# One mask for the 16 heads of a unit, and the output decay of a unit moved behind the mask of the next

## The chip, the cores and the metric

The kernel runs on one core of a Trainium2 chip. Its engines work side by side, each through its own instructions in order: TensorE (PE; its weight loads are shown as PEld), VectorE (DVE), ScalarE (ACT), GpSimd (POOL) and SyncE (SP), which here issues the DMA transfers. They wait for one another through semaphores. The metric is the device time of one execution in microseconds (us); the median of the runs counts.

## What is computed

Inputs are r, k, v, w, a, b for 4 batches x 8 heads, 768 time steps and 40 columns. For each head a 40x40 state is carried through time, and its output is then the input of a small layer of four attention experts, of which each token uses two:

```
for t in range(768):
    y[:, :, t] = einsum('bhd,bhde->bhe', r_t, state)
    Sa = einsum('bhde,bhe->bhd', state, a_t)
    state = state * w_t[:, :, None, :] - einsum('bhd,bhe->bhde', Sa, b_t)
    state = state + einsum('bhd,bhe->bhde', v_t, k_t)
x = y.transpose(0, 2, 1, 3).reshape(4, 768, 320)
```

Each expert e is then a causal softmax attention over x with wq[e], wk[e], wv[e] and wo[e]; the four are summed with the weights of a gate that keeps about the two largest.

## The kernel before

`recurrence` computes y, `moe` the experts. Time is cut into 24 chunks of 32 steps (c); four chunks make a group (w, six of them; cw is the chunk within the group). Within a chunk the recurrence is turned into matrix products: a unit is one chunk of 16 heads (G is 0 or 1), so there are 48 units, u = 2c + G. For each unit `unit(u)` gives seven pieces:

- `s_k`: transposes of the prepared keys KB (one for both units of a chunk), copied to LS by ACT (L373)
- `s_g` (L380): products with the state R1, copied to GT by ACT (L383)
- `s_u` (L388): products of GT with the inverted triangle TT, copied into rows 32 to 63 of R2 by ACT (L390)
- `s_v` (L395): transposes of R2, copied to VU by ACT (L396)
- `s_f` (L401): eight products (two instructions each) of VU with RB into one PSUM bank `p_f`; VectorE multiplies them by the triangular mask into R2 (L404), the first four products by one instruction and the last four by a second
- `s_y` (L412): 16 products (two instructions each) of LS with R2 into the fixed PSUM tile PY: the next state and the output of the chunk. ACT copies the state part to R1 (L424); in the last chunk of a group VectorE does it with a factor (L422). VectorE multiplies the output part by the decays SC into XT (L425, "the decay"). In the last chunk of a group four DMAs store XT to xT in DRAM (L430)
- `s_t` (L438): transposes of the new state, copied to LS by ACT (L440)

The main loop (L527) goes through steps n and takes, by the table MAIN, `s_v` of unit n-1, `s_t` of n-3, `s_k`, `s_g` of n, `s_f` of n-1, `s_u` of n and `s_y` of n-1. Behind every piece it puts the jobs of a hand-written table (SIDE, SIDE1, SIDE2): the preparation of the next group in `prep` (scans and products on VectorE, flags on ACT, the kb products L294 on PE, which VectorE moves out of PSUM with a mask in L295; loads of EW, EA and EK by SP in L208; stores Ld in L299) and the inversion of the triangles in `invert` (L324 and L326 on VectorE and GpSimd, which read MT and LT, loaded from Ld in L312 and L313). Each engine's order is that of this program text (`manual_schedule`), so whatever stands behind a waiting instruction on its engine waits too. The state goes from `s_y` of a unit over L424 to `s_g` of the unit two later. PSUM tiles named `ps` and `pw` have two buffers each, PY one.

Of the kernel before, what the change touches and what calls it, by code (L numbers as in the profile page):

```python
# [9 lines left out]
OP = mybir.AluOpType  # L10
# [131 lines left out]
def recurrence(tc, ctx, I, xT, FL, CM, early, tail=None, KP=(11, 11, 11, 11, 11, 11)):  # L142
    nc = tc.nc
# [4 lines left out]
    V, A, T, PL = nc.vector, nc.scalar, nc.tensor, nc.gpsimd  # L148

    def ps(shape):  # L150
        return pp.tile(shape, F32, name="ps", tag="ps", bufs=2)
# [10 lines left out]
    ident, mask, maskn = CM[:, 0:128], CM[0:64, 128:160], CM[0:64, 160:192]  # L162
# [32 lines left out]
    hd = lambda t, d: t.rearrange("p (h d) -> p h d", d=d)  # L195
# [55 lines left out]
            zero(t[96:128, 0:1280])  # L251
            A.activation(hd(t[64:104, 0:1280], 40), ident[64:104, None, 64:104].to_broadcast([40, 32, 40]), AF.Copy)

    pm, behind = [0, False], []

    def prep(i):

# [98 lines left out]
    def unit(u):  # L356
        c, G = divmod(u, 2)
        w, cw = divmod(c, 4)
        h0 = 16 * G
        gl, tt, ls, r1, r2, rb, sc = GF[w % 2], TF[w % 2], LS[c % 2], R1[c % 2], R2[c % 2], RB[c % 2], SC2[(w * 2 + G) % 6]  # L360
        gt, vu, xt = GT[G], VU[0], XT[G]
# [36 lines left out]
        def s_f():  # L398
            p_f = ps([64, 16, 32])
            for P in range(8):  # L400
                T.matmul(p_f[:, 2 * P:2 * P + 2], vu[:, P, :], rb[:, 8 * G + P, :], start=True, stop=True)  # L401
                if P % 4 == 3:
                    x = slice(8 * (P // 4), 8 * (P // 4) + 8)
                    V.tensor_tensor(hd(r2[0:64, 1280 + 512 * G:1792 + 512 * G], 32)[:, x], p_f[:, x],  # L404
                                    mask[:, None, :].to_broadcast([64, 8, 32]), op=OP.mult)
        def s_y():
            a = r2[:, 0:40]
            for P, s in PS:
                h = h0 + 2 * P + s
                m = bass.AP(a.tensor, a.offset + 40 * h, [a.ap[0], [1280 - 8 * h, 2], [1, 40]])  # L410
                o = 80 * (P % 4)
                T.matmul(PY[64 * s:64 * s + 40, P // 4, o:o + 80].rearrange("q (x d) -> q x d", x=2), ls[:, h, :], m, start=True, stop=True,  # L412
                         tile_position=(0, 64 * s))
            py = PY[:, :, 0:320].rearrange("q b (p x d) -> q b p x d", p=4, x=2)
            for s in range(2):
                q = slice(64 * s, 64 * s + 40)
                if c < 23:
                    o = rn[64:104, 832 * G:832 * G + 832].rearrange("q (b p e) -> q b p e", b=2, p=4)[:, :, :, 64 * s:64 * s + 40]
                    st = py[q, :, :, 0]
                    if cw == 3:  # L420
                        pn = PC2[((c + 1) // 4 * 2 + G) % 6]
                        V.tensor_tensor(o, st, pn[q, :, :, None].to_broadcast([40, 2, 4, 40]), op=OP.mult)  # L422
                    else:
                        A.activation(o, st, AF.Copy)  # L424
            V.tensor_tensor(xt[:, :, 32 * cw:32 * cw + 32].rearrange("q (b p) t -> q b p t", b=2), py[0:104, :, :, 1, 0:32],  # L425
                            sc.rearrange("q b (p c) t -> q b p c t", p=4)[:, :, :, cw, 0:32], op=OP.mult)
            if cw == 3:
                for g in range(2):
                    for s in range(2):
                        nc.sync.dma_start(xT.rearrange("b (p s e) t -> b s e p t", s=2, e=40)[2 * G + g, s, :, :, 128 * w:128 * w + 128],  # L430
                                          xt[64 * s:64 * s + 40, 4 * g:4 * g + 4])
        def s_t():
            if c == 23:
                return
# [4 lines left out]
            def copy(s):  # L439
                A.activation(ln[64:104, h0 + s:h0 + 16:2].rearrange("q (b p) e -> q b p e", b=2),  # L440
                             p_t[64 * s:64 * s + 40, :, 0:416].rearrange("q b (p e) -> q b p e", p=4)[:, :, :, 64:104], AF.Copy)
            behind.extend(lambda s=s: copy(s) for s in range(2))
        return dict(k=s_k, g=s_g, u=s_u, v=s_v, f=s_f, y=s_y, t=s_t)


    jobs = {}
    NU = 48
    MAIN = [("v", -1), ("t", -3), ("k", 0), ("g", 0), ("f", -1), ("u", 0), ("y", -1)]

    def at(n, s, *fs):  # L450
        n = max(n, 0)
        x = ("f" if s <= 3 else "u") if n % 2 == 0 else ("u" if s <= 2 else "y")
        q = jobs.setdefault((n // 2, x), [])
        q.extend(((n, s), f) for f in fs)
# [5 lines left out]
    P = [prep(i) for i in range(24)]  # L460
# [63 lines left out]
            for z in part.split():  # L524
                at(n, k, lambda z=z: seq(z))
    pm[1] = True
    for n in range(NU + 1):  # L527
        if n == 40:
            early.close()
            for k, s, f in tail(KB[4:]) if tail else []:  # L530
                at(k, s, f)
        for x, d in MAIN:
            if x == "k":
                if n % 2 == 0 and n < NU:
                    units[n if n % 4 == 0 else n - 1]["k"]()
            elif 0 <= n + d < NU:
                units[n + d][x]()
            while x == "g" and behind:
                behind.pop(0)()
            if n and x == ("y" if n % 2 else "k"):  # L540
                load_c((n + 3) // 2, 2 * (n % 2))
            if n and n % 2 == 0 and x == "y":
                load_c((n + 3) // 2, 1)
            for _, f in sorted(jobs.get((n, x), []), key=lambda z: z[0]):
                f()
# [427 lines left out]
```

## Time and profile before

| | before |
|---|---|
| runs | 750.51, 739.98, 752.2 us; median 750.51 |
| profiled execution | 748.43 us, span of the trace 746.6 |
| PE / PEld busy | 586.2 (79%) / 508.2 (68%) |
| DVE busy | 491.1 (66%) |
| ACT busy | 463.6 (62%) |
| POOL busy | 336.0 (45%) |
| chain that ended last | PE 45%, DVE 22%, ACT 14%, DMA 7% |

All times of the profile are from the start of the span. Busy time is time in which an engine executes; matmuls are pipelined, so PE's is no measure of its peak. PEclk is the clock that TensorE was granted, as a share of full speed. A wait is put down to the engine that released it last. The chain that ended last is followed back from the last instruction of the execution.

### The profile page before, as it was taken

Reading aid. Unit: us, or ns where it says so; the run is one execution under the profiler, and the core shown is the slowest. Engines: PE = TensorE matmul, PEld = TensorE weight load, DVE = VectorE, ACT = ScalarE, POOL = GpSimd, SP = SyncE. Lnnn points to the kernel's source line nnn. Section 1 sums busy time; section 2 is a strip of 40 time slices with the busy share of each in tenths; the row PEclk is TensorE's granted clock in tenths of the full one; section 3 lists DMA queues with packets and bytes.
Section 4 is the critical chain, followed back from the end, with each engine's and each line's share of the span. In section 5 each row is a group of like instructions: output and inputs, shape, how many; then the busy total and the mean of one; then the engine's idle time right before and its main releaser. Section 6 shows DMA issues by size and latency. Waiting matters only on the chain.

```text
span 746.6 us, 21791 instructions
## 1 busy us (share of the span) xinstructions
PE 586.2 (79%) x8801; PEld 508.2 (68%) x8801; DVE 491.1 (66%) x1155; ACT 463.6 (62%) x1018; POOL 336.0 (45%) x512
## 2 busy tenths in 40 slices
PE   4530677785778767877798888879989989999996
PEld 4520666685668667866687777778778777877774
DVE  8899777745755586568656533239898678658751
ACT  6793477555666756675666766746656556656753
POOL 5465288217812683168307600114556244532641
PEclk9565699978889988998899999999999999999999
DMA  7861573457445843684445283143113212111101
GB/s 186 202 155 40 124 172 94 111 103 185 106 123 112 204 105 102 131 207 106 107 84 157 84 203 102 34 138 95 45 51 93 51 42 78 54 40 43 36 28 49
DMA packets 88548, 78.10 MB, mean 105 GB/s; under 512 B 54776, under 2 KB 72952, under 8 KB 88440
## 3 DMA queue, kind: packets, MB, share of 16 engines
q1 hardware_dynamic: 88296, 76.54, 41.5%
q8 instruction: 71, 1.16, 0.7%
q14 instruction: 37, 0.30, 0.1%
q10 hardware_dynamic: 144, 0.10, 0.0%
HBM read 56.17 MB, written 14.16 MB: 94 GB/s over the span
## 4 chain that ended last, share of the span: by engine, by line
PE 45%; DVE 22%; ACT 14%; DMA 7%; issue 5%; SPq 0%; POOL 0%; ACTq 0%; DVEq 0%; POOLq 0%
PE ot L857 5%; PE sc L809 4%; PE ps L401 4%; PE pt L731 4%; DMA EK<-in_EK 4%; PE pt L839 4%; PE pt L866 3%; DVE MT L326 3%; PE py L412 3%; PE pt L750 3%; PE ps L380 3%; DVE TP L324 3%; PE pw L294 2%; PE pw L368 2%; PE ps L388 2%
## 5 line engine op out<-in xcount | busy, mean ns | idle before, releaser
L831 POOL TENSOR_TENSOR P<-P,m 128x128 f32<-128x128 f32 (+2 forms) x96 | 87.7, 935 | 103.0 <-DVE m L827 51.8
L401 PE MATMUL ps<-RB,VU 128*64 128x64 f32 x768 | 70.3, 240 | 51.1 <-DVE R L404 47.5
L404 DVE TENSOR_TENSOR R<-ps,CM 64x256 f32<-64x256 f32 x96 | 39.9, 415 | 101.9 <-PE ps L401 101.9
L401 PEld LDWEIGHTS ps<-RB,VU 128*64 128x64 f32 x768 | 57.7, 150 | 59.0 <-DVE R L404 54.3
L326 POOL TENSOR_TENSOR MT<-MT,TP 128x84 f32<-128x84 f32 (+13 forms) x169 | 85.8, 508 | 13.2
L383 ACT ACTIVATE GT<-ps 32x320 f32<-32x320 f32 x96 | 41.0, 428 | 70.5 <-PE ps L380 69.7
L820 ACT ACTIVATE P<-sc,m 128x128 f32<-128x128 f32 (+2 forms) x96 | 60.8, 634 | 31.9 <-DVE m L819 25.9
L819 DVE TENSOR_REDUCE m<-sc 128x1 f32<-128x128 f32 (+2 forms) x96 | 59.4, 622 | 27.3 <-PE sc L812 25.8
L412 PE MATMUL py<-R,LS 128*40 128x80 f32 x1536 | 71.8, 249 | 3.7 <-ACT LS L373 3.7
L390 ACT ACTIVATE R<-ps 32x320 f32<-32x320 f32 x96 | 41.2, 429 | 43.6 <-PE ps L388 42.6
L809 PE MATMUL sc<-ks,qs 128*128 128x384 f32 (+4 forms) x256 | 64.4, 353 | 4.5 <-ACT P L820 4.2
L412 PEld LDWEIGHTS py<-R,LS 128*40 128x40 f32 x1536 | 63.3, 128 | 5.1 <-ACT LS L373 5.0
L324 POOL TENSOR_TENSOR TP<-LT,MT 128x220 f32<-128x220 f32 (+9 forms) x100 | 52.1, 521 | 7.8
L839 PE MATMUL pt<-CM,P 128*128 128x128 f32 x336 | 51.9, 276 | 2.4 <-ACT pt L845 2.0
L368 PE MATMUL pw<-CM,KB 104*128 104x104 f32 x192 | 24.8, 278 | 36.4 <-DVE GL L295 24.6
L294 PE MATMUL pw<-AB,KB 104*64 104x64 f32 x672 | 49.5, 238 | 1.9 <-DVE GLe L295 1.8
L388 PE MATMUL ps<-GT,TT 128*33 128x40 f32 x1536 | 46.9, 217 | 4.1 <-DVE GL L295 4.1
L809 PEld LDWEIGHTS sc<-ks,qs 128*128 128x128 f32 x256 | 41.2, 191 | 12.1 <-ACT P L820 9.8
L395 PE MATMUL pw<-CM,R 66*80 66x66 f32 x384 | 33.0, 232 | 20.2 <-issue 14.6
L396 ACT ACTIVATE VU<-pw 80x512 f32<-80x512 f32 x48 | 28.5, 594 | 32.6 <-PE pw L395 31.8
L294 PEld LDWEIGHTS pw<-AB,KB 104*64 104x64 f32 x672 | 47.2, 153 | 2.2 <-DVE GLe L295 2.0
L368 PEld LDWEIGHTS pw<-CM,KB 104*128 104x128 f32 x192 | 19.8, 152 | 40.5 <-DVE GL L295 24.7
(151 smaller groups left out, 1460.2 us busy)
## 6 DMA issues: line engine op xcount, KB each, us to landing
RB<-in_RB SPq DMA_DIRECT2D x24, 320.0 KB
EK<-in_EK SPq DMA_DIRECT2D x18, 416.0 KB
ks<-ks SPq DMA_DIRECT2D x32, 192.0 KB
R<-in_VG SPq DMA_DIRECT2D x24, 208.0 KB
EW<-in_EA SPq DMA_DIRECT2D x18, 214.5 KB
R<-in_VT SPq DMA_DIRECT2D x48, 80.0 KB
R<-in_RT SPq DMA_DIRECT2D x24, 160.0 KB
xT<-XT SPq DMA_DIRECT2D x48, 80.0 KB
```

Source lines behind the costliest of these rows:

```text
L294: T.matmul(p_a[:, p, cc, :], kb[0:104, n, :], AB[0:104, n, :], start=True, stop=True)
L324: return [lambda: e.tensor_tensor(tmp, row[:, None, :].to_broadcast([128, m, n]), M[:, r0:r0 + m, j][:, :, None].to_broadcast([128, m, n]) ...
L326: lambda: e.tensor_tensor(o, o, tmp, op=OP.add)]
L368: T.transpose(p_k[:, g, 128 * p:128 * p + 104], KB[(w * NG + 2 * G + g) % NKB][0:104, p * 4 + cw:p * 4 + cw + 2, :].rearrange("q c k -> q ...
L388: T.matmul(p_u[64 * s:64 * s + 33, P], tt[:, o:o + 33], gt[:, P, s], start=True, stop=True, tile_position=(0, 64 * s))
L401: T.matmul(p_f[:, 2 * P:2 * P + 2], vu[:, P, :], rb[:, 8 * G + P, :], start=True, stop=True)
L412: T.matmul(PY[64 * s:64 * s + 40, P // 4, o:o + 80].rearrange("q (x d) -> q x d", x=2), ls[:, h, :], m, start=True, stop=True, tile_positi ...
L809: T.matmul(ps[:, c, 0:cw], QS[b][:, e, o], KS[b][:, e, z, k], start=(z == 0), stop=(z == 1 and not last), skip_group_check=True)
L819: V.tensor_reduce(m[:, 0, t:t + 1], ps[:, 0:ch, 0:cw], axis=AX.XY, op=OP.max, negate=True)
L820: later(DE, lambda: A.activation(pv, ps[:, 0:ch, 0:cw], AF.Exp, bias=m[:, 0, t:t + 1], accum_out=m[:, 1, t:t + 1]))
L831: PL.tensor_tensor(P[:, 0:n], P[:, 0:n], m[:, 3, t:t + 1].to_broadcast([128, n]), op=OP.mult)
L839: T.transpose(p[:, 128 * y:128 * y + 128], st["P"][t][:, 128 * c:128 * c + 128], ident)
```

## The change

`s_f` masks all 16 heads of the unit with one VectorE instruction behind the eighth product. `s_y` no longer issues the decay and the stores: it puts them into a list `late`, which the main loop empties right behind `s_f` of the next step. The loop runs one step longer, for the last decay.

```
-    pm, behind = [0, False], []
+    pm, behind, late = [0, False], [], []
...
                 T.matmul(p_f[:, 2 * P:2 * P + 2], vu[:, P, :], rb[:, 8 * G + P, :], start=True, stop=True)
-                if P % 4 == 3:
-                    x = slice(8 * (P // 4), 8 * (P // 4) + 8)
-                    V.tensor_tensor(hd(r2[0:64, 1280 + 512 * G:1792 + 512 * G], 32)[:, x], p_f[:, x],
-                                    mask[:, None, :].to_broadcast([64, 8, 32]), op=OP.mult)
+            V.tensor_tensor(hd(r2[0:64, 1280 + 512 * G:1792 + 512 * G], 32), p_f, mask[:, None, :].to_broadcast([64, 16, 32]), op=OP.mult)
...
-            V.tensor_tensor(xt[:, :, 32 * cw:32 * cw + 32].rearrange("q (b p) t -> q b p t", b=2), py[0:104, :, :, 1, 0:32],
-                            sc.rearrange("q b (p c) t -> q b p c t", p=4)[:, :, :, cw, 0:32], op=OP.mult)
-            if cw == 3:
...
+            def decay():
+                V.tensor_tensor(xt[:, :, 32 * cw:32 * cw + 32].rearrange("q (b p) t -> q b p t", b=2), py[0:104, :, :, 1, 0:32],
+                                sc.rearrange("q b (p c) t -> q b p c t", p=4)[:, :, :, cw, 0:32], op=OP.mult)
+                if cw == 3:
...
+            late.append(decay)
...
-    for n in range(NU + 1):
+    for n in range(NU + 2):
...
                 units[n + d][x]()
+            while x == "f" and late:
+                late.pop(0)()
```

The lines of the changed kernel move with it: the mask is L402, `s_y`'s products L409, the factor copy L419, ACT's state copy L421, the decay L423, the stores L428.

On TensorE, one step of the main loop with its waits (R and RB are a chunk's buffers, LS the weights of `s_y`). Before:

```order
L401 MATMUL ps<-RB_127,VU_126 64x64 [waits DMAHW3_49,Activation_49]
L401 MATMUL ps<-RB_127,VU_126 64x64 x3
L401 MATMUL ps<-RB_127,VU_126 64x64 [waits DVE_49]
L401 MATMUL ps<-RB_127,VU_126 64x64 x3
L388 MATMUL ps<-GT_132,TT_118 33x40 [waits PE_49,Activation_49]
L388 MATMUL ps<-GT_132,TT_118 33x40 x15
L412 MATMUL py<-R_124,LS_120 40x80 [waits DMAHW4_49,Activation_49]
L412 MATMUL py<-R_124,LS_120 40x80 [waits Activation_49]
L412 MATMUL py<-R_124,LS_120 40x80 x5
L412 MATMUL py<-R_124,LS_120 40x80 [waits DVE_49]
```

and of the change, the same step:

```order
L401 MATMUL ps<-RB_127,VU_126 64x64 [waits DMAHW3_49,Activation_49]
L401 MATMUL ps<-RB_127,VU_126 64x64 x7
L388 MATMUL ps<-GT_132,TT_118 33x40 [waits PE_49,Activation_49]
L388 MATMUL ps<-GT_132,TT_118 33x40 x15
L409 MATMUL py<-R_124,LS_120 40x80 [waits DMAHW4_49,DVE_49,Activation_49]
L409 MATMUL py<-R_124,LS_120 40x80 [waits Activation_49]
L409 MATMUL py<-R_124,LS_120 40x80 x14
```

The wait for VectorE in the middle of `s_f` is gone, and the one in `s_y` has moved from its eighth product to its first.

On VectorE, the end of a chunk group, steps with kb products (`-` before, `+` the change; XT is the decay's output, GLe that of the kb products' mask, R that of the mask or of the state's factor copy):

```order
-L404 TENSOR_TENSOR R_125<-ps,CM 64x256 x2
+L402 TENSOR_TENSOR R_125<-ps,CM 64x512
+L423 TENSOR_TENSOR XT_130<-py,SC_93 104x8x32
 L279 TENSOR_TENSOR AB_111<-EA_82,SC_97 40x16x32
 L295 TENSOR_TENSOR GLe<-pw,CM 64x4x128 x2
-L422 TENSOR_TENSOR R_122<-py,PC_88 40x8x40 x2
-L425 TENSOR_TENSOR XT_129<-py,SC_92 104x8x32
+L419 TENSOR_TENSOR R_122<-py,PC_88 40x8x40 x2
 L270 SCALAR_TENSOR_TENSOR SUF_85<-EW_81,D_79 104x528
 L272 COPY PC_86<-SUF_85 104x4
 L274 RECIPROCAL D1P_84<-PC_86 104x4
```

Two masks have become one, the decay of the unit before follows it, and the unit's own decay no longer stands behind the state's factor copy and ahead of the scan.

On SP's queue, the stores of one XT at the end of a chunk group (TT, R, Ld and EK are loads and stores of the jobs and of `load_c`):

```order
 L332 DMA TT_119<-Td_136 32x32x32 x4
-L430 DMA xT<-XT_129 40x4x128 x4
-L350 DMA R_125<-in_VT 32x640
-L299 DMA Ld_133<-GLe 32x32x32
-L348 DMA R_123<-in_VG 32x1664
+L350 DMA R_125<-in_VT 32x640
+L299 DMA Ld_133<-GLe 32x32x32
+L348 DMA R_123<-in_VG 32x1664
+L428 DMA xT<-XT_129 40x4x128 x4
 L208 DMA EK_83<-in_EK 104x1024
```

The four stores have moved behind three other transfers and stand directly ahead of the load of EK.

## Rows read from the trace of the kernel before

**Rows 1.** Waits of all engines: engine, line, whom for: us in all, times, longest.
```profile
PE ps L401 <- DVE R L404: 47.5, 48, 5.4
```

**Rows 2.** Timeline, an undisturbed step: start us, us, engine line op out<-in, [idle before].
```profile
442.38 0.65 PE L401 MATMUL ps<-RB,VU 128*64 128x64 f32 x8
442.60 0.87 ACT L383 ACTIVATE GT<-ps 32x320 f32<-32x320 f32 x2 [0.77 <-PE ps L380]
443.07 0.42 DVE L404 TENSOR_TENSOR R<-ps,CM 64x256 f32<-64x256 f32 x1 [1.91 <-PE ps L401]
...
443.54 0.62 PE L401 MATMUL ps<-RB,VU 128*64 128x64 f32 x7 [0.51 <-DVE R L404]
...
443.94 0.22 PE L388 MATMUL ps<-GT,TT 128*33 128x40 f32 x1
...
444.58 0.24 PE L412 MATMUL py<-R,LS 128*40 128x80 f32 x1
...
444.62 1.28 PE L412 MATMUL py<-R,LS 128*40 128x80 f32 x31
```

**Rows 3.** Timeline of VectorE: the first and the last of the 15 late masks.
```profile
89.62 0.39 DVE L404 TENSOR_TENSOR R<-ps,CM 64x256 f32<-64x256 f32 x1
...
417.67 0.41 DVE L404 TENSOR_TENSOR R<-ps,CM 64x256 f32<-64x256 f32 x1
```

**Rows 4.** Timeline, a step whose mask is late.
```profile
199.86 0.68 PE L401 MATMUL ps<-RB,VU 128*64 128x64 f32 x8
...
202.46 0.41 DVE L404 TENSOR_TENSOR R<-ps,CM 64x256 f32<-64x256 f32 x1
...
204.78 0.35 PE L412 MATMUL py<-R,LS 128*40 128x80 f32 x1
...
204.90 1.85 PE L412 MATMUL py<-R,LS 128*40 128x80 f32 x31
```

**Rows 5.** Windows: length; busy of PE, PEld, DVE, ACT, POOL; PEclk; DMA; GB/s.
```profile
202.90:206.80 3.90, 3.88 (x74) 3.77 (x75) 2.47 (x7) 1.61 (x4) 3.16 (x9) 0.59 0.23 54
442.30:446.00 3.70, 3.19 (x97) 2.94 (x92) 0.83 (x2) 2.62 (x7) 0.00 (x0) 1.00 0.79 210
```

**Rows 6.** Groups by shape (busy, mean ns | idle), then timeline of VectorE.
```profile
L295 DVE TENSOR_TENSOR GL<-pw,CM 64x512 f32<-64x512 f32 x22 | 14.6, 677 | 6.7 <-PE pw L294 6.7
...
218.54 1.27 DVE L295 TENSOR_TENSOR GL<-pw,CM 64x512 f32<-64x512 f32 x2
...
439.69 1.01 DVE L422 TENSOR_TENSOR R<-py,PC 40x320 f32<-40x320 f32 x2 [1.28 <-PE py L412]
...
440.73 0.43 DVE L425 TENSOR_TENSOR XT<-py,SC 104x256 f32<-104x256 f32 x1
```

**Rows 7.** Timeline of ScalarE in a step with `s_k`: first and last of eight rows.
```profile
342.50 0.87 ACT L383 ACTIVATE GT<-ps 32x320 f32<-32x320 f32 x2 [1.73 <-PE ps L380]
...
348.37 0.59 ACT L396 ACTIVATE VU<-pw 80x512 f32<-80x512 f32 x1
```

**Rows 8.** Timeline of VectorE behind a second mask.
```profile
212.61 0.42 DVE L404 TENSOR_TENSOR R<-ps,CM 64x256 f32<-64x256 f32 x1 [0.77 <-PE ps L401]
212.95 0.22 DVE L326 TENSOR_TENSOR MT<-MT,TP 128x75 f32<-128x75 f32 x1
```

**Rows 9.** Timeline of VectorE, a load it waits for.
```profile
258.56 1.76 DVE L284 TENSOR_TENSOR KB<-EK,SUF 104x512 f32<-104x512 f32 x2 [0.32 <-DMA EK<-in_EK]
```

**Rows 10.** Timeline of TensorE, `s_v` behind a step with kb products.
```profile
231.94 0.63 PE L395 MATMUL pw<-CM,R 66*80 66x66 f32 x8 [1.87 <-issue]
```

**Rows 11.** Timelines of SP's queue, VectorE and GpSimd around one EK load.
```profile
233.82 0.39 SPq L208 DMA_DIRECT2D EK<-in_EK  x1
...
236.95 0.42 DVE L404 TENSOR_TENSOR R<-ps,CM 64x256 f32<-64x256 f32 x1 [4.52 <-PE ps L401]
...
238.64 3.08 POOL L281 TENSOR_TENSOR KB<-EK,SUF 104x1024 f32<-104x1024 f32 x1 [22.09 <-DVE R L404]
...
248.47 0.16 POOL L315 MEMSET MT<- 128x32 f32 x1 [5.47 <-DMA MT<-Ld]
```

More of the change, by code (lines that the diff above doesn't have):

```diff
@@ L424, in s_y @@
                         A.activation(o, st, AF.Copy)
-            V.tensor_tensor(xt[:, :, 32 * cw:32 * cw + 32].rearrange("q (b p) t -> q b p t", b=2), py[0:104, :, :, 1, 0:32],
-                            sc.rearrange("q b (p c) t -> q b p c t", p=4)[:, :, :, cw, 0:32], op=OP.mult)
-            if cw == 3:
[L428 to L431, printed above, removed]
+            def decay():
+                V.tensor_tensor(xt[:, :, 32 * cw:32 * cw + 32].rearrange("q (b p) t -> q b p t", b=2), py[0:104, :, :, 1, 0:32],
+                                sc.rearrange("q b (p c) t -> q b p c t", p=4)[:, :, :, cw, 0:32], op=OP.mult)
+                if cw == 3:
+                    for g in range(2):
+                        for s in range(2):
+                            nc.sync.dma_start(xT.rearrange("b (p s e) t -> b s e p t", s=2, e=40)[2 * G + g, s, :, :, 128 * w:128 * w + 128],
+                                              xt[64 * s:64 * s + 40, 4 * g:4 * g + 4])
+            late.append(decay)
         def s_t():
```

## The prediction

> **What bounds the kernel now.** I read the page first (busy shares, then the 40 slices), then the list of waits, then the timeline of single steps in the part in which the 48 units run. No engine is busy throughout there: the units are a chain that goes round TensorE (PE), ScalarE (ACT) and VectorE (DVE), one unit per step. So the change is worth what it takes out of a step's chain, not what it takes off DVE's busy time.
>
> The list of waits has one entry that belongs to this change alone [rows 1]: PE waits 48 times for L404, 47.5 us in all, once in every step. It stands in the middle of `s_f`: the fifth product may not be written into the PSUM bank while DVE masks the first four.
>
> A step without other trouble is [rows 2]. Set its first product at 0. The first four products take 0.65, the mask starts at 0.69 and ends at 1.11, the second four start at 1.16 (0.05 after the mask), `s_u` at 1.56, and `s_y` at 2.20, as soon as `s_u` is issued. The second mask lies beside `s_u`. The wait there is 0.51; 48 of those would be 24.5 us, so the other 23.0 us come from steps in which DVE comes late to the mask. There are 15 such steps, with the first mask 0.3 us or more late: the first and the last of these masks are in [rows 3]. [rows 4] is one: the mask starts at 202.46 instead of 200.55. In the stretch behind it the granted clock is 0.59, where the undisturbed step has 1.00 [rows 5], so nearer to 1.2 than to 2.4 GHz, and `s_y` takes 1.85 us.
>
> **The change part by part.** *One mask.* The 16 product instructions now run in one piece. Eight take 0.40 to issue (443.54 to 443.94), and a mask starts 0.69 behind the start of the eight that it waits for, so it starts at 0.40 + 0.69 = 1.09. `s_u` can start when both GT copies are done, 443.47 and 0.05, at 1.14: it gains 0.42. The price of a 64x512 mask is that of L295, the same form with a mask factor: 0.677 us [rows 6].
>
> *The decay behind it.* It is one DVE instruction of 0.42 per unit, of the unit before. It reads PY, which `s_y` writes, and the rows of the built order show the one wait of `s_y` on DVE moved to its first matmul, with the decay ahead of it. So `s_y` waits for mask and decay. How soon the decay follows is bounded on both sides: two L295 in a row take 1.27 for 0.68 each, so the second starts 0.59 behind the first; L425 behind L422 starts 0.03 after its end, 0.71 for a mask [rows 6]. I take 0.59, because mask and decay, like two L295, both start at partition 0, while the second L422 starts at partition 64. The Trainium skill, page "VectorE: DVE Perf Modes", section "Two Vector instructions with no wait between them", says that a Vector instruction is held until the earlier ones are finished when its operands start in another group of 32 partitions than the last ones in that memory, and otherwise starts earlier; both rows agree, and by it the value is also 0.59.
>
> So behind a mask `s_y` can start 0.59 + 0.42 + 0.05 = 1.06 later. In an undisturbed step that is 1.09 + 1.06 = 2.15 (2.27 by the other bound) against 2.20: **nothing gained, -0.05 to +0.07**. The 0.42 that `s_u` gains is spent in front of `s_y`. I count 0.
>
> *Late steps.* Before, `s_y` starts 1.51 behind the first mask in a fast step (443.07 to 444.58) and 2.32 in a slow one (202.46 to 204.78); now 1.06. By the timeline 7 of the 15 are slow: 7 x 1.26 = 8.8. Of the other 8, four are steps with `s_k`, in which ACT works without a gap from the GT copy to the VU copy that the next `s_f` waits for (342.50 to 348.96, [rows 7]); a sooner `s_y` gives nothing there. The other four: 4 x 0.45 = 1.8. Together **10.6**.
>
> *DVE gets free sooner.* From the first mask to DVE's next work it was 0.42 + 0.77 + 0.34 = 1.53 [rows 2, 8]; now it is 0.59 and the decay, which is only moved. That is 0.94 per step, plus any wait of the decay. It counts only where the next mask is late from DVE's own work: the steps whose first products stand at about 118, 200, 275 and 349 us. The one at 200 is 1.9 late [rows 4], the others by the timeline about as much or more; I take 0.94 and a further 0.35 from the step before, whose own lateness or decay wait goes too: 4 x 1.3 = **5.2**. Where a load makes DVE late, as EK does at 258.56 [rows 9], nothing comes earlier.
>
> *Steps with kb products (L294) between `s_u` and `s_y`.* In the last three steps of a chunk group L294 fills PE between the two, so `s_y` is held by PE, not by DVE, and the 0.42 of `s_u` stays: 8 steps x 0.42 = 3.4. In 8 steps DVE had the decay in front of the L295 that empty the PSUM which the next `s_v` waits for (1.87 us at 231.94, [rows 10]); it goes from there: 8 x 0.34 = 2.7. Together **6.1**.
>
> *Last unit.* No `s_u` stands there, so `s_y` could start at 1.56 and now starts at 2.15: **-0.6** (a loss). The last decay stands where it stood.
>
> *The stores, on SP's queue.* The decay of every fourth pair issues four stores of xT. They move too: behind VT, Ld and VG, and they now wait for a decay behind the next unit's mask. EK is issued behind them. Before, EK was issued at 233.82 and POOL's KB started 4.8 later. Now: mask at 236.95 + 0.40, decay done 1.01 later at 238.4, four issues at the 0.39 that EK's own takes, EK at about 240, **6 us later**. What covers it: POOL's next fixed date is MT at 248.47, 9.8 behind KB's start, with KB itself (3.08) and one more product between [rows 11]. So the cover is about used up, and the EA load behind that product may slip, and with it the mask behind 258.56. The second set of stores moves out from in front of RB, RT and EA, which helps EA. In three windows the cost lies between 0 and 3 x 6; I take 1.3 each, since the cover in the row is nearly as long as the delay: **-4**.
>
> **Sum.** 10.6 + 5.2 + 6.1 - 0.6 - 4 = 17.3 us. The profiled execution took 748.43 (span 746.6); that gives 731.1, and I predict **731 us**. Against the median of the runs shown, 750.51, it would be 2.6% less, against the profiled run 2.3%.
>
> **The rivals.**
> *A: the wait only moves.* ACT or POOL set the step wherever DVE and PE come sooner, so that the 5.2 and the 6.1 are lost. For it: ACT's gapless step [rows 7]. Against it: in the late slow steps ACT waits for PE behind the mask. 748.4 - 10.6 + 4.6 = 742.4. Within 2%.
> *B: the load chain gives it all back (slower).* EK 6 us late passes on to the Ld store and the MT load behind it, and in all four windows to the mask that waits for EK. 4 x 6 lost against 21.9 - 0.6 = 21.3 gained: 748.4 - 21.3 + 24 = 751.1. It decides from 21.3 / 4 = 5.3 us per window on. Against it: the 6.75 between the end of KB and MT.
> *C: the clock comes back.* With shorter waits the slow steps stay at the upper level. `s_y` then takes 1.28 as in [rows 2] instead of the 1.85 of [rows 4]: 0.57 in each of 7 steps, 4 us, and without the loss on loads 731.1 - 8 = 723. The Trainium skill, page "TensorE: Matmul & The Clock Gate", section "Part 1: The HAM clock gate", says that the throttled clock is the default and activity releases it, which would be this; the 0.59 behind the late mask agrees. Against C: three of the seven are late from loads, and there the wait in front of `s_y` remains.
>
> **How the numbers follow.** Forecast (725 to 738) 0.47; A 0.33; C 0.12; B 0.08. The range reaches to C at 722 and to just past A at 744; beyond it lie B and the tails of A and C, 2 in 10. Differences of 2% are about what a measurement of this kernel can tell from no change (its three runs lie between 739.98 and 752.2). Faster by over 2% means under 735.5: most of the forecast's case (0.39), C (0.12) and little of A: 0.52. Slower by over 2% means over 765.5, for which B would have to cost 9.6 us in each window: 0.05 with what I may have overlooked. Within 2%: 0.43.
>
> **What would show it.** The waits of L401 on the mask are gone from the list. A wait of `s_y` (L409) on DVE appears, about 0.4 us in undisturbed steps, 1 us or more in late ones, and `s_y` starts 2.15 to 2.27 behind the first product there. The mask takes 0.68, the decay starts 0.59 behind it and no longer waits for L421. The undisturbed steps keep their period; the steps at 118, 200, 275 and 349 us lose 2 to 3 us each. EK is issued about 6 us later against its step, and POOL's KB with it. I am wrong if undisturbed steps get longer by more than 0.1 (then the decay is dearer than here), if the masks behind EK come later against their step by more than 2 us (B), or if the late steps lose less than 1 us (A).

## The result and the profile after

The change is worth about 1%: 736.19 us (median of 20 runs) against 742.85 us of the kernel before, timed in turn with it (20 runs); the ratio is 0.9894, with a 95% interval from 0.986 to 0.9927. That is within 2%. (The ratio leaves out six runs of the change that lie more than 1.5% above its fastest one; the two medians alone would give 0.991.) Predicted were 731 us, a range from 722 to 744, and chances of 0.52 for faster, 0.43 for the same and 0.05 for slower.

The profiled execution took 742.62 us, near the upper end of what the changed kernel needs (729.09 to 744.53). Since two of its executions differ by more than the change brings, I read two traces of it: this first one, and a second one of 730.14 us (below). From the page of the first, the span, the busy times (behind each engine its share of the span and its instructions) and the granted clock in the 40 slices (tenths of full speed):

```profile
span 740.5 us, 21727 instructions
PE 596.9 (81%) x8801; PEld 517.7 (70%) x8801; DVE 491.1 (66%) x1107; ACT 463.3 (63%) x1018; POOL 341.0 (46%) x512
PEclk8675688889789977898799999999999999999999
```

The line that the change aimed at, PE waiting 48 times for the first half mask [rows 1], is gone. The groups of the three lines concerned (busy, mean ns of one | idle ahead of them, and what ended it):

```profile
L401 PE MATMUL ps<-RB,VU 128*64 128x64 f32 x768 | 60.8, 239 | 3.7 <-ACT VU L396 3.5
L402 DVE TENSOR_TENSOR R<-ps,CM 64x512 f32<-64x512 f32 x48 | 32.7, 681 | 112.5 <-PE ps L401 112.4
L409 PE MATMUL py<-R,LS 128*40 128x80 f32 x1536 | 66.3, 240 | 41.8 <-issue 10.5 <-ACT LS L373 8.2 <-DVE XT L423 5.0
```

The 3.7 us that are left on L401 belong to other waits; 41.8 us now stand in front of `s_y` (L409). The undisturbed step, the first of the group without kb products that [rows 2] showed, now reads (timeline: start, us, engine, line):

```profile
437.89 1.12 PE L401 MATMUL ps<-RB,VU 128*64 128x64 f32 x16
...
439.02 0.77 PE L388 MATMUL ps<-GT,TT 128*33 128x40 f32 x32
439.04 0.68 DVE L402 TENSOR_TENSOR R<-ps,CM 64x512 f32<-64x512 f32 x1 [2.74 <-PE ps L401]
439.65 0.41 DVE L423 TENSOR_TENSOR XT<-py,SC 104x256 f32<-104x256 f32 x1
...
440.16 1.06 PE L409 MATMUL py<-R,LS 128*40 128x80 f32 x25 [0.37 <-ACT LS L439]
```

The mask starts 1.15 behind the first product, the decay 0.61 behind the mask, `s_y` 2.27 behind the first product, 0.37 of it idle. The row names L439, but that copy (438.99, 0.89 long) was done at 439.88; the decay was done at 440.06. It is the decay that `s_y` waits for.

To see where the time went, I take the distance from the first product of `s_f` of one unit to that of the next (47 of them, units 0 to 47) in each trace and add them up by what disturbs the step: units 0, 4, 12, 20 and 28, whose mask is late from VectorE's own work; 2, 10, 18 and 26, where it is late from a load; the twelve steps 5 to 7, 13 to 15, 21 to 23 and 29 to 31 with or behind kb products; 1, 34, 36 and 42, single late steps; the other 22. All in us:

| kernel | VectorE 5 | load 4 | kb 12 | single 4 | other 22 | all 47 |
|---|---|---|---|---|---|---|
| before | 54.1 | 43.7 | 129.4 | 28.8 | 146.3 | 402.3 |
| the change, first trace | 46.5 | 47.1 | 128.6 | 26.3 | 146.7 | 395.2 |
| the change, second trace | 45.8 | 45.7 | 119.0 | 26.3 | 146.8 | 383.6 |
| one_mask | 46.9 | 34.0 | 128.0 | 25.5 | 144.7 | 379.1 |
| late_only | 52.5 | 46.9 | 128.7 | 28.2 | 150.6 | 406.9 |
| ahead | 50.7 | 35.6 | 121.2 | 25.5 | 145.4 | 378.4 |
| stores_behind | 48.7 | 38.0 | 130.2 | 26.3 | 146.7 | 389.8 |
| ahead_sb | 48.3 | 35.7 | 119.5 | 25.5 | 144.9 | 373.9 |
| fill | 49.5 | 35.4 | 132.0 | 26.3 | 146.7 | 389.9 |
| loads_later | 44.4 | 48.0 | 124.8 | 26.3 | 146.8 | 390.2 |
| fill6 | 45.5 | 42.2 | 116.7 | 26.3 | 146.8 | 377.6 |
| before_fill6 | 51.5 | 40.8 | 120.9 | 27.1 | 147.9 | 388.3 |
| ahead_fu_l2 | 51.3 | 32.3 | 122.3 | 25.5 | 144.9 | 376.3 |
| all_parts | 49.0 | 31.7 | 116.4 | 25.5 | 144.9 | 367.5 |

Three things stand in the first three rows. The five steps with a late VectorE give back 8 us. The load steps *lose* 3.4 and 2.0, all of it at unit 2 (8.7 before, 13.4 in both traces; units 10, 18 and 26 take 35.0 before, 33.7 and 32.2 now). And the kb steps are as before in one trace and 10 us shorter in the other, with the same program. The column *other* does not move, and *single* falls by 2.5.

Each row is one execution, so some caution is needed. `fill6` and `before_fill6` (below) add work to six kb steps alone; outside these they are the change and the kernel before once more, and their load columns are 42.2 against 47.1 and 45.7, and 40.8 against 43.7, their VectorE columns 45.5 against 46.5 and 45.8, and 51.5 against 54.1. A difference of some 3 us in one of these two columns (5 in the load column) is nothing by itself.

### The profile page after: what moved, and what is told of

Read it like the earlier page. It is cut to its first block, busy times and chain, and to the rows that moved or that the text cites. A ratio compares the mean times of both kernels' runs of the same rounds, so it can differ in the third digit from the quotient of the medians.

```text
span 740.5 us, 21727 instructions
## 1 busy us (share of the span) xinstructions
PE 596.9 (81%) x8801; PEld 517.7 (70%) x8801; DVE 491.1 (66%) x1107; ACT 463.3 (63%) x1018; POOL 341.0 (46%) x512
## 4 chain that ended last, share of the span: by engine, by line
PE 47%; ACT 22%; DVE 13%; issue 7%; DMA 4%; SPq 1%; POOL 1%; DVEq 0%; ACTq 0%; POOLq 0%
PE ot L858 5%; PE py L409 5%; PE ps L380 4%; PE sc L810 4%; PE pt L732 4%; ACT LS L439 4%; PE pt L840 4%; ACT GT L383 4%; PE pt L867 3%; PE pw L368 3%; PE pw L437 3%; ACT R L390 3%; PE pw L294 3%; ACT R L421 3%; PE pw L395 2%
## 5 line engine op out<-in xcount | busy, mean ns | idle before, releaser
L402 DVE TENSOR_TENSOR R<-ps,CM 64x512 f32<-64x512 f32 x48 | 32.7, 681 | 112.5 <-PE ps L401 112.4
L409 PE MATMUL py<-R,LS 128*40 128x80 f32 x1536 | 66.3, 240 | 41.8 <-issue 10.5
L326 POOL TENSOR_TENSOR MT<-MT,TP 128x84 f32<-128x84 f32 (+13 forms) x169 | 86.4, 511 | 13.2
L409 PEld LDWEIGHTS py<-R,LS 128*40 128x40 f32 x1536 | 58.1, 120 | 45.8 <-issue 19.0
L820 DVE TENSOR_REDUCE m<-sc 128x1 f32<-128x128 f32 (+2 forms) x96 | 59.4, 622 | 27.6 <-PE sc L813 26.3
L401 PE MATMUL ps<-RB,VU 128*64 128x64 f32 x768 | 60.8, 239 | 3.7 <-ACT VU L396 3.5
L401 PEld LDWEIGHTS ps<-RB,VU 128*64 128x64 f32 x768 | 55.4, 153 | 4.7 <-ACT VU L396 4.6
L324 POOL TENSOR_TENSOR TP<-LT,MT 128x220 f32<-128x220 f32 (+9 forms) x100 | 53.4, 534 | 7.8
L421 ACT ACTIVATE R<-py 40x320 f32<-40x320 f32 x72 | 31.0, 430 | 34.9 <-PE py L409 28.0
L294 PE MATMUL pw<-AB,KB 104*64 104x64 f32 x672 | 50.5, 241 | 2.7 <-DVE GLe L295 1.7
L368 PE MATMUL pw<-CM,KB 104*128 104x104 f32 x192 | 27.9, 301 | 29.7 <-DVE GL L295 24.5
L395 PE MATMUL pw<-CM,R 66*80 66x66 f32 x384 | 35.9, 245 | 18.9 <-issue 12.7
L294 PEld LDWEIGHTS pw<-AB,KB 104*64 104x64 f32 x672 | 48.0, 155 | 3.4 <-DVE GLe L295 1.8
L437 PE MATMUL pw<-CM,R 104*104 104x104 f32 x368 | 49.8, 289 | 0.1
L281 POOL TENSOR_TENSOR KB<-EK,SUF 104x1024 f32<-104x1024 f32 x5 | 10.9, 2187 | 84.6 <-DMA EK<-in_EK 53.2
L810 PEld LDWEIGHTS sc<-ks,qs 128*128 128x128 f32 x256 | 40.8, 189 | 12.6 <-ACT P L821 9.3
```

Of the source, the lines that this page charges most:

```text
L294: T.matmul(p_a[:, p, cc, :], kb[0:104, n, :], AB[0:104, n, :], start=True, stop=True)
L324: return [lambda: e.tensor_tensor(tmp, row[:, None, :].to_broadcast([128, m, n]), M[:, r0:r0 + m, j][:, :, None].to_broadcast([128, m, n]) ...
L326: lambda: e.tensor_tensor(o, o, tmp, op=OP.add)]
L437: T.transpose(p_t[0:104, P // 4, 104 * (P % 4):104 * (P % 4) + 104], rn[0:104, o:o + 104], ident[0:104, 0:104])
L810: T.matmul(ps[:, c, 0:cw], QS[b][:, e, o], KS[b][:, e, z, k], start=(z == 0), stop=(z == 1 and not last), skip_group_check=True)
L820: V.tensor_reduce(m[:, 0, t:t + 1], ps[:, 0:ch, 0:cw], axis=AX.XY, op=OP.max, negate=True)
```

## The experiments

The theory after the result: the one mask gains in late steps; the decay's new place costs, in front of `s_y` and through the stores that follow it onto SP's queue; the kb steps hang on the clock (`before_fill6` will show that this is not all of it). All kernels were timed in turn with the kernel before.

### One half of the change each, and the decay on the other side of the mask

**after_again**: the changed kernel, unaltered.

> The changed kernel once more, for a second trace beside the others. Theory 1 (late steps gain, loads lose): 0.985 to 0.994 of the time before, and the same two places lose again: the product of EK that VectorE makes near the step at 326 us waits 3 to 4 us for its load, which stands behind the four stores of xT on SP's queue, and the step at 100 us has its mask 3 us or more late. Theory 2 (these losses are chance of one execution): the waits of KB on EK are back at 1 us or less, and the step at 100 us is as before.

731.62 us against 742.19, ratio 0.9865 (0.9816 to 0.9914). Unit 2 again has its mask 3.7 us late, and KB near unit 26 waits 3.35 us for EK: both losses are there in both traces. The wait for EK belongs to the change: VectorE's KB waits 2.65 to 3.95 us for EK at each of units 10, 18 and 26 in both traces (and 2.67 to 3.31 in `fill6`), but 1.77, 0.32 and 0.22 before. (In `fill`, whose steps 15 and 23 are 2.2 longer, it is 2.90, 0.48 and 1.39.) For unit 2 two traces are too few, as will be seen at `loads_later`.

**one_mask**: the decay stays behind its own step.

```diff
-            late.append(decay)
+            decay()
```

> One mask per unit, the decay stays behind its own step. Theory 1 (what gains is the mask, and what loses is that the decay and with it the stores move): undisturbed steps have s_y at 1.89 instead of 2.20 behind the first product (1.16 + 0.68 + 0.05), the stores of xT stand where they stood, so EK waits as before; 12 even steps x 0.31 = 3.7 and 7 late steps x 1.3 = 9 gained, nothing lost on loads: about 730 us, 0.983, better than the whole change. Theory 2 (the decay that holds VectorE in front of its other work makes the masks late, and moving it is what gains): late masks stay as late as before, at least 2 us from 1.9 at the step at 200 us, and the time is 738 to 743, 0.993 to 1.0.

725.30 us against 742.19, by the medians 0.977 (one of its six runs took 712.91, the others 724.49 to 727.90, so there is no interval): better than the whole change (731.62 beside it), and better than expected. The step of [rows 2], in this kernel, has no idle in front of `s_y`, which follows `s_u` 1.94 behind the first product:

```profile
422.38 1.12 PE L401 MATMUL ps<-RB,VU 128*64 128x64 f32 x16
...
423.53 0.68 DVE L402 TENSOR_TENSOR R<-ps,CM 64x512 f32<-64x512 f32 x1 [2.56 <-PE ps L401]
...
424.32 0.86 PE L409 MATMUL py<-R,LS 128*40 128x80 f32 x18
```

The VectorE steps take 46.9, as with the change (46.5 and 45.8): the mask alone gains as much in them as the whole change, and the decay's place adds nothing that these sums show. The load steps take 34.0 instead of 46 to 47.

**late_only**: two half masks as before, the decay behind the next step's second one.

```diff
+                if P % 4 == 3:
+                    x = slice(8 * (P // 4), 8 * (P // 4) + 8)
+                    V.tensor_tensor(... [:, x], p_f[:, x], mask ... [64, 8, 32], op=OP.mult)
-            V.tensor_tensor(..., p_f, mask ... [64, 16, 32], op=OP.mult)
```

> Two masks per unit as before, the decay behind the next step's second mask. Theory 1: s_y waits for the second mask and the decay, 1.88 + 0.35 + 0.42 + 0.05 = 2.70 instead of 2.20, 0.5 in 12 even steps = 6 lost, the 0.3 that VectorE waits ahead of the decay saved in the late steps, some 4 gained, the loads lose 4: 749 us, 1.008. Theory 2 (the decay's place is what gains): 737 to 740, 0.992 to 0.996.

754.48 us, ratio 1.0152 (1.0115 to 1.0189): the decay's move by itself makes the kernel slower. The loss is larger than expected (1.008). The undisturbed steps lose (150.6 against 146.3), the load steps lose 3.2, and the VectorE steps win 1.6 of the 5.2 that I had put down to this half, which is no more than two executions of the kernel before differ by (54.1 and, in `before_fill6`, 51.5).

**ahead**: the decay of the unit before ahead of the mask, not behind it.

```diff
+            while x == "f" and late:
+                late.pop(0)()
             ... units[n + d][x]()
-            while x == "f" and late:
-                late.pop(0)()
```

> As the change, but the decay of the unit before stands ahead of the next step's mask instead of behind it. Theory 1 (in undisturbed steps the decay of 0.41 stands in front of s_y): s_y starts 1.89 instead of 2.27 behind the first product; 0.38 in 12 even steps = 4.5 gained against the change, nothing in late steps where mask and decay only change places: about 732 us, 0.985 of before. Theory 2 (ScalarE or TensorE sets the step wherever s_y comes sooner): s_y at 1.89 but the periods as in the change, 736 us, 0.990.

723.84 us, ratio 0.9738 (0.9698 to 0.9778), 8 us better than the change. `s_y` starts 1.94 behind the first product, but the undisturbed steps give only 1.4 us and the single ones 0.8 (the period goes from 6.62 to 6.38, then something else sets it): the expected 4.5 were too much. The gain lies in the load steps, 35.6 instead of 45.7. There the decay, and with it the stores and EK behind them, no longer wait for a mask. About half as much is lost again in the VectorE steps (50.7 instead of 45.8), three of which follow load steps. SP's queue and VectorE at unit 10, first of `ahead` (unit 8 starts at 159.30):

```profile
161.38 2.86 SPq L428 DMA_DIRECT2D xT<-XT  x4
164.28 0.69 SPq L208 DMA_DIRECT2D EK<-in_EK  x1
```
```profile
171.16 1.63 DVE L284 TENSOR_TENSOR KB<-EK,SUF 104x512 f32<-104x512 f32 x2
```

and then of the change (second trace, unit 8 starts at 160.15):

```profile
166.59 2.22 SPq L428 DMA_DIRECT2D xT<-XT  x4
168.86 0.44 SPq L208 DMA_DIRECT2D EK<-in_EK  x1
```
```profile
175.45 2.00 DVE L284 TENSOR_TENSOR KB<-EK,SUF 104x512 f32<-104x512 f32 x2 [3.37 <-DMA EK<-in_EK]
```

EK is issued 5.0 behind the start of unit 8 there, 8.7 here, and the wait for it is gone there.

### The order of stores and loads on SP's queue

**stores_behind**: as the change, with the stores of a decay issued at the end of the next `s_u`.

```diff
-                if cw == 3:
-                    ... four nc.sync.dma_start(xT ..., xt ...)
+            def store(): ... the same four
+            if cw == 3:
+                out.append(store)
...
+            while x == "u" and out:
+                out.pop(0)()
```

> As the change, but the four stores of xT that follow a decay are issued at the end of the next step's s_u, so that both loads of EK that had them in front no longer do. Theory 1 (the stores in front of EK cost what the prediction put at 4 us): VectorE's product KB near the step at 318 us (unit 26) waits under 1.5 us for EK instead of 3.4, its mask is 1 to 2 us late instead of 2.3, and the time is 728 us, 3 to 4 below the change. Theory 2 (EK's date is set by the transfers themselves and by the buffers, not by its place on SP's queue): the wait stays at 3 us and the time at 731 to 732.

731.77 us against 743.94, ratio 0.9811 (0.9754 to 0.9868), no different from the change within the intervals. But the load steps are 7.7 to 9.1 shorter than in the two traces of the change (38.0 in all). At units 10 and 26 of this kernel:

```profile
177.14 1.91 DVE L284 TENSOR_TENSOR KB<-EK,SUF 104x512 f32<-104x512 f32 x2 [0.15 <-DMA EK<-in_EK]
...
321.91 1.75 DVE L284 TENSOR_TENSOR KB<-EK,SUF 104x512 f32<-104x512 f32 x2 [1.53 <-DMA EK<-in_EK]
```

0.15 and 1.53 instead of 3.37 and 3.35. Units 10, 18 and 26 take 25.0 here, 33.7 and 32.2 in the change and 30.9 in `fill6`, where the stores stand as in the change. So the stores in front of EK cost these steps 6 to 9 us, about twice what I had reckoned; my first theory holds at its place and fails in the total. Some 3 us go back at once, since the VectorE steps behind (12 and 28) grow (48.7 against 45.8), and this trace has long kb steps (130.2), which no store explains.

**loads_later**: as the change, with the loads of VT, RB and RT issued behind the next step's `s_f`.

```diff
-            if n and n % 2 == 0 and x == "y":
-                load_c((n + 3) // 2, 1)
+            if n > 1 and n % 2 and x == "f":
+                load_c((n + 2) // 2, 1)
```

> As the change, but the loads of VT (its second half), RB and RT for a later pair are issued after the next step's s_f instead of at the end of the step. Theory 1 (issued 2 us sooner than before, they share the DMA engines with the EA that VectorE waits 5.6 us for in the step at 100 us): EA lands 1 us or more sooner, the mask of that step is 2.7 us late instead of 3.7, time 729 to 731. Theory 2 (that EA comes when it comes, and only the step arrives sooner): mask 3.7 late as in the change, time 731 to 734.

738.15 us, ratio 0.9919 (0.9878 to 0.996). At unit 2 it does what the first theory says: the step takes 7.90 instead of 13.4. VectorE of the change (first trace) and of this kernel:

```profile
103.88 1.02 DVE L279 TENSOR_TENSOR AB<-EA,SC 40x512 f32<-40x512 f32 x1 [5.60 <-DMA EA<-in_EA]
```
```profile
99.63 0.68 DVE L279 TENSOR_TENSOR AB<-EA,SC 40x512 f32<-40x512 f32 x1 [2.69 <-DMA EA<-in_EA]
```

From its issue (94.30 and 92.96) EA takes 9.6 us there and 6.7 here. It is tempting to put the 3 us down to the 560 KB that no longer come beside it (80 of VT, 320 of RB, 160 of RT, by the page), but the other traces do not bear that out. `fill` (below) has these loads where the change has them, and its program is the change's up to unit 5; its EA, issued at 92.69, took 7.4:

```profile
100.08 0.84 DVE L279 TENSOR_TENSOR AB<-EA,SC 40x512 f32<-40x512 f32 x1 [3.56 <-DMA EA<-in_EA]
```

The five traces with the change's order (its own two, `stores_behind`, `fill`, `fill6`) have 9.6, 9.5, 9.3, 7.4 and 8.5 us for EA, and 13.4, 13.4, 13.0, 8.9 and 11.3 for unit 2; the kernel before and `before_fill6` have 8.0 and 8.4, and 8.7 and 11.8; the three kernels with the loads moved (`loads_later`, `ahead_fu_l2`, `all_parts`) 6.7, 8.0 and 7.2, and 7.9, 10.8 and 8.7. So moving the loads goes with a sooner EA, by some 1.5 us on average, but the ranges overlap, and how much of the loss at unit 2 belongs to the change is not shown.

The same loads now stand in front of EK at units 10, 18 and 26, where KB waits 4.5 to 5.4 us for it, and those three steps take 40.1 instead of 32.2: the total is no better than the change's.

### The clock in the kb steps

The two traces of the change differ by 9.6 us there. TensorE ahead of unit 6, first and second trace:

```profile
137.78 1.07 PE L395 MATMUL pw<-CM,R 66*80 66x66 f32 x8 [2.36 <-issue]
...
140.17 1.28 PE L380 MATMUL ps<-R,GLe 128*33 128x40 f32 x32
```
```profile
136.68 0.63 PE L395 MATMUL pw<-CM,R 66*80 66x66 f32 x8 [2.37 <-issue]
...
138.08 0.77 PE L380 MATMUL ps<-R,GLe 128*33 128x40 f32 x32
```

The idle in front is equal to 0.01 us; behind it the clock falls in one execution and not in the other.

**fill**: 32 matmuls that nobody reads ahead of `s_v` of twelve units.

```diff
+            if x == "v" and n - 1 in (6, 7, 8, 14, 15, 16, 22, 23, 24, 30, 31, 32):
+                z = ps([128, 512])
+                for k in range(32):
+                    T.matmul(z[...40 rows, 0:80], CM[:, 0:40], CM[:, 0:80], ...)
```

> As the change, and TensorE gets 32 matmuls of 40x80 that nobody reads (1.3 us at the upper clock) in front of s_v in the 12 steps behind kb products, where it sat idle 1.7 to 2.7 us. It adds work and leaves none out. Theory 1 (the idle in front of s_v lets the granted clock fall in the steps with kb products, and this is most of the difference between two executions of the changed kernel, 33.6 against 29.9 us for units 21 to 23): the four stretches of units 5 to 7, 13 to 15, 21 to 23 and 29 to 31 show a granted clock of 0.98 or more and last 29 to 31 us each, together 116 to 119; time 726 to 730. Theory 2 (the clock there does not hang on this idle): clocks of 0.8 to 0.95 as in the change, time 731 to 737. If the added matmuls hold s_v up, 12 x 1 us are lost: 743.

735.25 us, ratio 0.9895 (0.9861 to 0.993). `s_v` of all twelve units takes 0.66 or less, so the clock stays; but the filling takes 2.5 to 4.1 us (each of its matmuls is two instructions, which I had forgotten in the 1.3), more than the idle, and in front of units 7, 16, 24, 31 and 32 there had been none. Units 7, 15, 23 and 31 are 0.9 to 2.2 longer, and the kb steps come to 132.0. Too much of it.

**fill6**: 16 of them, ahead of units 6, 14, 15, 22, 23 and 30 alone.

> As the change, with 16 matmuls of 40x80 that nobody reads (0.64 us for 32 passes of 40 columns, some 1.3 us in the rows of the larger filling) ahead of s_v in the six steps (units 6, 14, 15, 22, 23, 30) where TensorE sat idle 1.7 to 2.4 us. It adds work and leaves none out, and fits into the idle. Theory 1 (this idle lets the granted clock fall in the steps with kb products in some executions): s_v of the twelve units takes 0.70 or less, the four stretches show 0.95 or more and last together 116 to 121 instead of 119 to 129; time 726 to 729. Theory 2 (the clock there hangs on something else): s_v of some of these units still takes 1.0 or more; time 731 to 736.

725.98 us against 747.22, ratio 0.9756 (0.9705 to 0.9807). The windows of units 5 to 7, 13 to 15, 21 to 23 and 29 to 31 (length; busy of PE, PEld, DVE, ACT, POOL; granted clock; DMA), of the change in the first trace and of this kernel:

```profile
129.51:164.88 35.37, 29.15 (x531) 27.56 (x525) 21.02 (x41) 19.69 (x39) 8.15 (x18) 0.81 0.48 106
207.16:237.43 30.27, 25.03 (x531) 23.34 (x525) 19.36 (x36) 19.68 (x39) 2.70 (x5) 0.94 0.55 128
279.92:313.53 33.61, 28.90 (x528) 27.75 (x523) 19.04 (x35) 19.68 (x39) 2.27 (x3) 0.79 0.44 102
357.25:386.62 29.37, 25.80 (x528) 24.18 (x523) 15.78 (x30) 18.05 (x35) 2.00 (x1) 0.91 0.45 101
```
```profile
126.12:158.12 32.00, 26.17 (x562) 24.45 (x557) 20.92 (x41) 19.71 (x39) 10.11 (x22) 0.95 0.53 117
200.06:228.98 28.92, 25.87 (x594) 24.09 (x589) 19.35 (x36) 19.71 (x39) 2.85 (x5) 1.00 0.55 129
271.15:299.81 28.66, 25.88 (x594) 24.09 (x589) 19.12 (x35) 19.71 (x39) 3.06 (x6) 1.00 0.59 132
340.77:367.93 27.16, 24.78 (x562) 23.01 (x557) 15.81 (x30) 18.08 (x35) 5.13 (x8) 1.00 0.53 113
```

Clocks of 0.95 and 1.00, 116.7 us in all, as the first theory said.

**before_fill6**: the same filling in the kernel before.

> The kernel before with the same filling. Theory 1 (what the filling gives has nothing to do with the change): the four stretches last 122 to 126 instead of 129.3, time 736 to 739, 0.992 of before. Theory 2 (only the change has idle of that kind at the edge): no difference, 742 to 744.

738.54 us against 747.22, ratio 0.9892 (0.9846 to 0.9939); the kb steps take 120.9 instead of 129.4. So this loss was there before the change and has nothing to do with it. The same four windows in this kernel:

```profile
128.82:161.68 32.86, 25.97 (x563) 24.21 (x557) 21.39 (x43) 19.69 (x39) 9.15 (x17) 0.95 0.55 123
203.50:233.55 30.05, 25.77 (x595) 24.07 (x589) 19.38 (x39) 19.69 (x39) 5.20 (x3) 1.00 0.56 125
276.86:306.63 29.77, 25.76 (x595) 24.07 (x589) 19.13 (x38) 19.68 (x39) 5.37 (x3) 1.00 0.56 129
350.01:378.28 28.27, 24.71 (x563) 23.01 (x557) 16.22 (x33) 18.05 (x35) 1.99 (x1) 1.00 0.45 102
```

These two filled kernels are the best comparison of the change with the kernel before, since the granted clock is the same in each of the four windows. The change shortens the kb steps by 4.2 us (120.9 to 116.7): by 0.40 to 0.45 in units 13, 21 and 29, by 0.67 to 0.71 in units 14, 22 and 30, by 0.86 in unit 6, and by nothing in the other five. At unit 13 (VectorE, then TensorE, first of `before_fill6`, unit start 203.50):

```profile
210.98 0.41 DVE L425 TENSOR_TENSOR XT<-py,SC 104x256 f32<-104x256 f32 x1
211.31 1.27 DVE L295 TENSOR_TENSOR GL<-pw,CM 64x512 f32<-64x512 f32 x2
```
```profile
212.08 0.63 PE L395 MATMUL pw<-CM,R 66*80 66x66 f32 x8 [1.57 <-issue]
```

and of `fill6` (unit start 200.06):

```profile
207.42 1.27 DVE L295 TENSOR_TENSOR GL<-pw,CM 64x512 f32<-64x512 f32 x2
```
```profile
208.19 0.63 PE L395 MATMUL pw<-CM,R 66*80 66x66 f32 x8 [1.11 <-issue]
```

Without the decay in front of it, L295 starts 0.45 sooner against the unit's start (7.81 to 7.36), and `s_v` behind it too (8.58 to 8.13). In all 47 steps this pair shows the change 10.7 us shorter: 6.0 in the VectorE steps, 4.2 in the kb steps, 0.8 and 1.1 in the single and the other ones, and a loss of 1.4 in the load steps.

### Parts together

**ahead_sb** is `ahead` and `stores_behind` together; **ahead_fu_l2** issues the first set of stores already behind the jobs of the next `s_f`, and moves the load of VT, RB and RT for unit 2 alone; **all_parts** adds the filling of `fill6`.

```diff
-            while x == "u" and out:
-                out.pop(0)()
+            while out and x == "fu"[out[0][0]]:
+                out.pop(0)[1]()
...
-            if n and n % 2 == 0 and x == "y":
-                load_c((n + 3) // 2, 1)
+            if n and n % 2 == 0 and x == "y" and n != 2 or n == 3 and x == "f":
+                load_c((n + 3 - n % 2) // 2, 1)
```

> Both at once: the decay ahead of the next step's mask, and the stores behind the next step's s_u. Theory 1 (the two act at different places and add): 720 us, 0.970 of before. Theory 2 (the loads set the dates that a sooner s_y runs into): 724 us as with the decay ahead alone, 0.975.

722.18 us, ratio 0.975 (0.9702 to 0.9797): not told apart from `ahead`. Its load steps were short already, and VectorE now waited 7.7 us, in three places, with a decay for the stores of the XT that it overwrites.

> Decay ahead of the next step's mask; stores of the first set behind EK at the end of the next step's s_f, those of the second set behind its s_u; and the loads of VT, RB and RT once, in the early part, issued after the next step's s_f. Theory 1 (the losses on loads are a matter of what stands ahead of a load on SP's queue): the step of unit 2 lasts 8 instead of 12.4 to 13.4, decays do not wait for stores of xT, the load steps 10, 18 and 26 stay under 9: 716 to 718, 0.965 of before. Theory 2 (what is won at unit 2 is given back at the next load): 722 as before, 0.972.

724.38 us against 747.22, ratio 0.9689 (0.9641 to 0.9736). Load steps 32.3; but unit 2 takes 10.8, not 8, and kb steps 122.3. By the intervals it is not told apart from `ahead` (0.9698 to 0.9778).

> The same with the filling of six steps. Theory 1: 712 to 715, 0.960. Theory 2 (the filling costs what it gives): 716 to 720.

714.12 us against 747.22, ratio 0.9576 (0.9534 to 0.9619), which is what the first theory said and the best kernel here: 4.2% below the kernel before, 3% better than the change. `all_parts` against `ahead_fu_l2` is again the filling: 10 us by the medians, and 8.8 in the traces, of which 5.9 are in the kb steps and 2.1 at unit 2, which stands ahead of any filling.

## Why the prediction came out as it did

*What held.* The wait of L401 is gone. The mask takes 0.68, the decay follows 0.61 behind it, `s_y` starts 1.11 behind the start of a late mask (1.06 predicted; 200.41 to 201.52 in the rows of unit 12 below). The undisturbed steps gain nothing, for the reason given: what `s_u` gains is spent in front of `s_y`. The bound of 2.27 was met, not the 2.15 that I chose: all sixteen products take 1.12, not 1.05. The last unit loses 0.75 (0.6 predicted; 1.59 before, 2.34 now). The stores stand ahead of EK, and EK comes 5.8 us later against unit 15 (2.0 ahead of its start before [rows 11], 3.8 behind it in the second trace; 6 predicted).

*Late steps (10.6) and VectorE free sooner (5.2).* Measured: 7.6 and 8.3 in the five VectorE steps (6.0 in the filled pair), 2.5 in the single ones (0.8). The step that failed is the second: 5.2 for the decay's place. In the four steps for which it was forecast (units 4, 12, 20 and 28) `s_y` alone was to bring 4 x 1.26 = 5.0, together 10.2; they became 5.3 and 6.0 shorter (45.3 to 40.0 and 39.4), and 5.2 in the filled pair (44.3 to 39.1), that is 1.3 to 1.5 each and not 2 to 3. `late_only` shows 1.6, within what two executions differ by, and in `one_mask` the mask alone gains as much there as the change. At unit 12 the next mask comes 8.34 behind the last (8.64 before), although some 1.3 us of work and waiting should have gone from between (VectorE, then TensorE, first trace):

```profile
192.07 0.68 DVE L402 TENSOR_TENSOR R<-ps,CM 64x512 f32<-64x512 f32 x1 [1.36 <-PE ps L401]
...
196.32 0.47 DVE L326 TENSOR_TENSOR MT<-MT,TP 128x99 f32<-128x99 f32 x1
196.82 0.52 DVE L324 TENSOR_TENSOR TP<-MT 128x100 f32<-128x100 f32 x1
197.37 0.45 DVE L326 TENSOR_TENSOR MT<-MT,TP 128x100 f32<-128x100 f32 x1
...
200.41 0.67 DVE L402 TENSOR_TENSOR R<-ps,CM 64x512 f32<-64x512 f32 x1
```
```profile
201.52 1.76 PE L409 MATMUL py<-R,LS 128*40 128x80 f32 x32 [2.79 <-ACT JK L267]
```

VectorE works without a pause, and its eleven L324 and L326 take 4.38 us between the two masks, where the same number took 3.57 before; with 0.14 on the other products this is nearly what is missing. Why they are slower (GpSimd works on the same pair of lines at the time, before and now) was not tried.

*kb steps (6.1).* There, at two thirds of the size: 4.2 in the filled pair, where the clock is equal. At unit 13 L295 comes 0.45 sooner; 0.33 of it is the place of the decay (210.98 to 211.31), as forecast (0.34). The 0.42 of `s_u` came only in the second step of a stretch (`s_y` of unit 14 starts 0.51 sooner, at 3.52 instead of 4.03) and not in the two others: at unit 13 `s_y` starts at 2.74 and 2.75, ahead of L294, and unit 15 takes 7.55 and 7.56. The 10 us that the second trace of the change wins there and the first does not go with the clock, which is 0.81, 0.94, 0.79 and 0.91 in the four windows of the first and 0.95, 1.00, 0.94 and 0.94 in the second. This was rival C in another place: I had looked for it in the late steps, where nothing came of it (0.82 in units 10 to 12 of the second trace, 0.84 before). Two of the seven slow steps, not three, are late from loads: at unit 0 VectorE works without a pause ahead of the mask.

*The stores (−4).* Right mechanism, mis-sized at its place: `stores_behind` puts it at 6 to 9 us, 2 to 3 per window instead of 1.3, before the 3 us that the steps behind give back. That is rival B at half strength (it needed 5.3 per window).

*Not foreseen.* Unit 2 loses 4.8 in both traces of the change. Its step starts 1.5 and 2.5 us sooner than before, but VectorE gets its EA 2.3 and 1.3 later (103.88 and 102.92 against 101.61). VT, RB and RT are issued sooner by the faster steps and run beside it; that this is the cause is not shown, since the filled pair shows no such loss (11.8 before, 11.3 now). And the executions of one kernel differ by 10 us from the clock.

So 17.3 us were forecast; the second trace has 18.7 less and the first 7.1 less in the steps, for other reasons than mine in part: 8 from VectorE steps, 2.5 from single ones, 3.4 and 2.0 lost on loads, and 0.7 and 10.3 from the kb steps, where the clock adds to or hides the 4 of the change. The filled pair, with the clock equal in the kb steps, has 10.7. The medians are 6.7 and 10.6 us apart in the two comparisons. So the change brought some 7 to 11 of the 17.3. The measured time is inside the range, 5 us above the middle, and on the side of the 2% to which I had given 0.43. That it lies so near is in part luck: I had set the sum against a profiled execution of 748.43, 5.6 above the median of before, and from that median the same sum would have given 725.6.

## What to carry over

Two edits in one change can pull against each other: here the single mask was worth more than the whole (16.9 us against 10.6, by the medians of one round), and moving the other instruction gave over a third of it back; time each alone. An instruction that fills a buffer for a store takes that store's place on the DMA queue along, so ask which load stands behind the store. When executions of one program differ by more than the change, split the time by kind of step first, and compare steps that had the same clock; and before a cause is given to a difference between two traces, see how far two executions of the same program differ at that step.

## What was not expected of the hardware

Behind an idle of 2.36 and of 2.37 us ahead of the same instruction, the granted clock fell in one execution and stayed up in the other (`s_v` 1.07 and 0.63 us). Matmuls without a reader, 1.4 us of them in six places, kept `s_v` of all twelve units at 0.66 or less, and were worth 1.1% in the kernel before, and 8 to 10 us in the changed one too (0.9756 of the time before against 0.9865 and 0.9894); the engine had more to do and was done sooner. After one of them (unit 6 of `fill6`, an idle of 1.76 left; 0.92 over the step) the clock fell all the same, so the filling makes the fall rare, not impossible.
